# A transformer block pair on one core: an explicit list of order, engines and PSUM banks in place of a planner's priority table

## The chip, the cores and the metric

The kernel runs on 1 core of one Trainium2 chip. The metric is the device time of one execution in microseconds; the median of three runs counts.

## The reference

Two identical layers are applied twice to x (2048 tokens, 512 channels, bf16). Each layer is a windowed causal attention and an MLP, both behind a layernorm without learned scale:

```python
H = 32; Dh = D // H; W = 256                    # 32 heads of 16 channels, window of 256 keys
qkv = (x @ wqkv).reshape(B, S, 3, H, Dh)...
scores = einsum("bhqd,bhkd->bhqk", q, k) * Dh ** -0.5
mask = (i - j >= 0) & (i - j < W)
o = softmax(where(mask, scores, -1e9)) @ v ... @ wo          # attention A
h = gelu(x @ w1 + b1); y = h @ w2 + b2                       # MLP B, 512 -> 1792 -> 512
x = x + A(layernorm(x)); x = x + B(layernorm(x)); and both once more
```

## The kernel before

X (16 tiles of 128 tokens), all weights and all intermediate results stay in SBUF. The two applications are unrolled into 32 token tiles `tau` (16 for each), worked in 16 blocks `b` of two tiles. The steps of a block and the names by which the profile shows them are these.

- `layernorm`: statistics (`BATCH_NORM_STATS2` into `stat`, L786), mean and variance (`statmv`, L788), `veps` (L790), all on DVE; the power -0.5 on POOL (`rstd`, L793); the normalized tile `xn` (L796) on DVE. For attention `xn` is transposed by TensorE and copied into `xnTA` by DVE (L769) or ACT (L771). For the MLP most tiles go another way: DVE transposes into `xs_`, a DMA writes it to a scratch tensor `scr_x`, and four DMAs read it back into `xnTB` (L808, L810), all on the SP queue.
- `lnq`, `kv`: projections against `Wqkv_sb`, groups `q…`, `k…`, `v…`, and their evacuations into `QT`, `Va` (DVE, L769, or ACT, L771) and `KT` (DVE alone, L882, 128x1024).
- `attention`: 152 score groups ("visits", `QT,KT` matmuls of 32x64 tiles) into four PSUM banks each, two exponentials per group on ACT into the ring buffer `E` (L971; 304 in all), masks on `E` by DVE or POOL (L994), then `pv` groups (`E,Va` matmuls of 64x17 tiles), whose result is transposed (`TT`, L1059), divided (`Rc`, `TM`, L1062, L1064) and transposed again into `OT` (L1069).
- `outproj` against `Wo_sb`, and `residual` (`X`, L842).
- `mlp`: ten jobs of two or four tiles. W1 groups, gelu on ACT (L1133, L1143; ACT switches its function table between exp and gelu), W2 groups `W_sb,gT`, residual. For six of a job's fourteen W1 groups DVE adds the bias first (L1130) and one gelu serves two groups.

Three kinds of matmul groups therefore stand on TensorE: full-array groups (128x128), score groups (32x64 tiles) and pv groups (64x17 tiles).

Every engine runs a fixed sequence. It is made at build time: each step is `add`ed to `PL`, a `_Plan`, with its engine or engines, a duration, what it reads and writes, a priority and a class of PSUM banks. `_Plan.run` is a list scheduler: at each moment an idle engine takes the ready step with the smallest priority, where `TUNE` adds a number of its own to the priority of each step and leans the choice between two engines. Four classes of banks (`sc`, `o`, `od`, `m1`) limit which groups may use which banks; steps can also have `after`: other steps that must be planned earlier (the gates between score groups, exponentials, W1 groups and gelus). `_Sched` then turns the resulting order into the engines' programs: semaphore waits come only from what a step reads and writes, from the banks, and from `behind`, which keeps a long POOL instruction behind the last DVE instruction that uses the same port. `after` and the priorities leave no trace in the program but the order.

The loads stand at the head of the SP queue: X tiles 0-1, X 2-3, the three blocks of Wqkv (Q, K, V), b1, X 4-7, then Wo, b2, W1, X 8-15 and W2 (b2 ahead of Wo in the program).

Of the kernel before, what the change touches and what calls it, by code (L numbers as in the profile page):

```python
# [55 lines left out]
class _Sched:  # L56
# [4 lines left out]
    COUNTERS = ("pe", "act", "dve", "pool") + tuple("spdma%d" % i for i in range(N_DMA_SEMS))  # L61
# [27 lines left out]
    def op(self, eng, fn, reads=(), writes=(), inc=1, dma=False, start=0.0, end=0.0, n=1, joins=(), behind=None):  # L89
# [8 lines left out]
        if dma:  # L98
            assert eng == "sp"
            counter = "spdma%d" % (self.dma_rr % self.N_DMA_SEMS)  # L100
            self.dma_rr += 1
            inc = 16
            need(counter, self.cnt_val[counter])
# [28 lines left out]
    def wait_all_dma(self, eng):  # L132
        waits = [(c, v) for c, v in self.cnt_val.items() if c.startswith("spdma") and v]
        self.prog[eng].append(dict(fn=None, waits=waits))
# [52 lines left out]
class _Plan:  # L187
# [5 lines left out]
    TURN = {}  # L193
    LINGER = 0.0
    CODE = (194.0, 256.0, 2.003, 3300.0)

    def __init__(self, pools, tune=((), ())):
        self.keys = {}
        self.tune = tune
        self.nodes = []  # L200
        self.lw = {}
        self.lr = {}
        self.pools = pools

    def add(self, eng, fn, dur, reads=(), writes=(), prio=0.0, alloc=None, free=(), after=(), geo=None, table=None,
            dma=False, alt=(), war=(), lock=False, joins=(), chain=False):

        i = len(self.nodes)
        k = self.keys.setdefault((eng, round(prio, 3), dur), len(self.keys))
        step, lean = (float(t[k]) if k < len(t) else 0.0 for t in self.tune)  # L210
        prio += step
        alt = tuple((e2, f2, d2, h2 + 4.0 * lean) for e2, f2, d2, h2 in alt)
# [14 lines left out]
        if free and eng == "dve":  # L227
            prio -= 1000.0
        self.nodes.append(dict(
            eng=eng, fn=fn, dur=dur, reads=list(reads), writes=list(writes), prio=prio, joins=tuple(joins),  # L230
            jdeps=frozenset(self.lw[r] for r in joins),
            alloc=alloc, free=tuple(free), deps=deps, geo=geo, table=table, dma=dma, lock=lock,
            alts=((eng, fn, dur, 0.0),) + alt, key=k, done=False, behind=None, then=None,
            heavy=any(a[0] == "pool" and a[2] > 600.0 for a in ((eng, fn, dur),) + alt),
        ))
        if eng == "pe":
            c = _Count()
            fn(c, _Anywhere())
            self.nodes[i]["n"] = c.n
        if chain:  # L240
            self.nodes[i - 1]["then"] = i
        return i

    def run(self):
        import heapq
        nodes = self.nodes
        n = len(nodes)
        succ = [[] for _ in range(n)]
        indeg = [0] * n
        for i, nd in enumerate(nodes):  # L250
            indeg[i] = len(nd["deps"])
            for d in nd["deps"]:
                succ[d].append(i)
        engs = ("pe", "act", "dve", "pool", "sp")
        rtime = {e: [0.0] * n for e in engs}
        pend = {e: [] for e in engs}
        ready = {e: [] for e in engs}
        efree = {e: 0.0 for e in engs}
        locked = {"dve": 0.0, "pool": 0.0}
        last_lock = {"dve": None, "pool": None}  # L260
        held = {e: None for e in engs}
        for nd in nodes:
            nd["chained"] = False
        for nd in nodes:
            if nd["then"] is not None:
                nodes[nd["then"]]["chained"] = True
        code, edge, loaded = 2.0, self.CODE[0], 0.0
        last_geo = None
        last_tab = "exp"
        bank_free = {}  # L270
        for cands in self.pools.values():
            for c in cands:
                for b in c:
                    bank_free[b] = True
        gmap = {}

        def fit(cls):
            for c in self.pools[cls]:
                if all(bank_free[b] for b in c):
                    return c  # L280
            return None

        for i in range(n):
            if indeg[i] == 0:
                for a in nodes[i]["alts"]:
                    heapq.heappush(pend[a[0]], (0.0, i))
        events = [(0.0, -1, None)]
        order = []
        busy = {e: 0.0 for e in engs}
        left = n  # L290
        seq = n
        while left:
            if not events:
                bad = [(nodes[i]["eng"], nodes[i]["writes"][:2], nodes[i]["alloc"]) for e in engs for (_, i) in ready[e] + pend[e]]
                raise RuntimeError("plan stuck with %d left: %s" % (left, bad[:12]))
            t = events[0][0]
            while events and events[0][0] <= t + 1e-9:
                _, _, act = heapq.heappop(events)
                if act is not None:
                    for b in act:  # L300
                        bank_free[b] = True
            for e in engs:
                while pend[e] and pend[e][0][0] <= t + 1e-9:
                    _, i = heapq.heappop(pend[e])
                    for a in nodes[i]["alts"]:
                        if a[0] == e:
                            if e == "pe":
                                ready[e].append((nodes[i]["prio"] + a[3], i))
                                if nodes[i]["geo"] == "c" and self.LINGER > 0.0:
                                    heapq.heappush(events, (rtime[e][i] + self.LINGER, seq, None))  # L310
                                    seq += 1
                            else:
                                heapq.heappush(ready[e], (nodes[i]["prio"] + a[3], i))
                if efree[e] > t + 1e-9 or not ready[e]:
                    continue
                pick = None
                if held[e] is not None:
                    if (held[e] in [x[1] for x in ready[e]]):
                        pick = held[e]
                elif e == "pe":  # L320
                    best = None
                    open_r = last_geo != "f" or any(
                        nodes[i]["geo"] == "r" and not nodes[i]["done"] and fit(nodes[i]["alloc"][0]) is not None for _, i in ready[e])
                    for p, i in ready[e]:
                        nd = nodes[i]
                        if nd["done"] or nd["chained"] or (nd["alloc"] is not None and fit(nd["alloc"][0]) is None):
                            continue
                        if nd["geo"] == "c" and not open_r and t < rtime[e][i] + self.LINGER:
                            continue
# [102 lines left out]
def bass_interleave_layers__sliding_block__dense_activation_gelu__prompt_kernel(  # L432
# [67 lines left out]
    def d_act(n):  # L500
        return n * 0.832 + 52
# [722 lines left out]
```

## Time and profile before

| | |
|---|---|
| three timed runs | 477.46, 478.22 (median), 479.47 us |
| profiled execution, its span from first to last instruction | 475.1 us |
| what lies around the span, taken from the median | 3.1 us |
| busy: PE, DVE, ACT, POOL | 450.4, 369.3, 396.2, 243.7 us |
| matmuls | 8793 |
| DMA queues | 16.92 MB on the queue of the kernel's own DMAs, 11.9% of 16 engines' span |

The profile gives no time for its execution other than the span, so the span stands for it, and the difference to the median of the timed runs, 3.1 us, is what lies around it. In the lists that follow, a line gives an engine, a line of the kernel, an operation, output<-input, the number of instructions and their time; what stands behind the last bar or in square brackets is the idle time of the engine just before, and what ended it. PE is TensorE's matmuls, PEld its weight loads. PEclk is the clock that TensorE was granted.

### The profile page before, as it was taken

The page shows a single profiled execution, that of the slowest core. Times are in us where ns is not written, and L with a number is a line of the kernel's source. Part 1 is how long each engine was busy: PE and PEld are TensorE (multiplying, and loading weights), DVE is VectorE, ACT ScalarE, POOL GpSimd, SP SyncE. Part 2 cuts the span into 40 slices and gives each one's busy share as a digit, 9 for nine tenths or more (in the row PEclk, how much of TensorE's full clock was granted, in tenths as well). Part 3 has the DMA queues.
Part 4 walks back from the last instruction along what each step waited for, and adds up shares of the span by engine and source line. Part 5 has one row for each costly group of instructions (what it writes and reads, how often), then busy time and mean ns, then how long its engine had stood idle before and what let it go on. Part 6 is the DMA issues. An engine that isn't in the chain of part 4 may idle for free.

```text
span 475.1 us, 19326 instructions
## 1 busy us (share of the span) xinstructions
PE 450.4 (95%) x8793; PEld 238.2 (50%) x8793; DVE 369.3 (78%) x735; ACT 396.2 (83%) x467; POOL 243.7 (51%) x275
## 2 busy tenths in 40 slices
PE   7987799999969999999989999999999999999997
PEld 4554464665433454645434545455455553454663
DVE  4999978988877688988878789797876958793611
ACT  2799999898897988879979898879998899875352
POOL 4296726843742435661778728672275816353200
PEclk9998999999977999999999999999999999999999
DMA  8910000001010100100010000101021001102000
GB/s 255 371 51 3 4 3 1 5 18 32 3 47 3 46 3 3 48 29 20 1 48 3 30 19 25 27 3 44 3 64 31 25 23 31 53 15 57 24 22 33
DMA packets 27837, 18.14 MB, mean 38 GB/s; under 512 B 15852, under 2 KB 27244, under 8 KB 27756
## 3 DMA queue, kind: packets, MB, share of 16 engines
q1 hardware_dynamic: 27756, 16.92, 11.9%
q8 instruction: 68, 1.11, 1.0%
q14 instruction: 13, 0.11, 0.1%
HBM read 11.41 MB, written 5.51 MB: 36 GB/s over the span
## 4 chain that ended last, share of the span: by engine, by line
PE 75%; DVE 13%; DMA 4%; ACT 4%; issue 1%; SPq 1%; POOL 1%; POOLq 0%
PE ps L32 73%; ACT E L971 3%; DVE KT L882 3%; DVE stat L786 3%; DVE X L842 2%; DMA X<-in_A_x_dram 2%; DMA xnTB<-scr_x 1%; PE ps L36 1%; DVE TT L1059 1%; DVE Va L769 1%; DMA scr_x<-xs_ 1%; DVE E L994 1%; DVE xn L796 1%; SPq L810 1%; DVE QT L769 1%
## 5 line engine op out<-in xcount | busy, mean ns | idle before, releaser
L971 ACT ACTIVATE E<-ps 128x1024 bf16<-128x1024 f32 x304 | 289.9, 1029 | 34.7 <-PE ps L32 32.8
L994 POOL TENSOR_TENSOR E<-E,mask 128x512 bf16<-128x512 bf16 (+1 forms) x148 | 154.6, 1064 | 114.1 <-ACT E L971 72.7
L32 PE MATMUL ps<-W_sb,gT 128*128 128x512 bf16 x448 | 114.9, 381 | 1.6 <-DMA xnTB<-scr_x 1.3
L32 PE MATMUL ps<-xnTB,W_sb 128*128 128x512 bf16 (+1 forms) x560 | 111.8, 340 | 1.1 <-DVE KT L882 0.5
L842 DVE TENSOR_TENSOR X<-X,ps 128x512 bf16<-128x512 bf16 x64 | 43.5, 681 | 45.3 <-PE ps L32 44.5
L32 PEld LDWEIGHTS ps<-xnTB,W_sb 128*128 128x128 bf16 x560 | 52.0, 98 | 46.5 <-issue 3.9
L32 PE MATMUL ps<-QT,KT 32*64 32x320 bf16 (+4 forms) x2976 | 66.7, 262 | 7.4 <-ACT E L971 3.4
L32 PE MATMUL ps<-xnTA,Wqkv_sb 128*128 128x256 bf16 x512 | 68.2, 277 | 3.2 <-DVE KT L882 1.2
L1143 ACT ACTIVATE gT<-ps,b1T 128x512 bf16<-128x512 f32 (+1 forms) x92 | 49.3, 587 | 23.0 <-PE ps L32 23.0
L32 PEld LDWEIGHTS ps<-W_sb,gT 128*128 128x128 bf16 x448 | 39.4, 97 | 48.9 <-issue 6.3
L793 POOL TENSOR_TENSOR rstd<-veps,mhalf 128x1 f32<-128x1 f32 x64 | 37.9, 602 | 40.3 <-DVE veps L790 38.5
L32 PEld LDWEIGHTS ps<-xnTA,Wqkv_sb 128*128 128x128 bf16 x512 | 46.8, 99 | 20.1 <-issue 4.4
L32 PEld LDWEIGHTS ps<-QT,KT 32*64 32x64 bf16 x2976 | 27.7, 104 | 53.1 <-ACT E L971 31.9
L32 PE MATMUL ps<-E,Va 64*17 64x128 bf16 (+3 forms) x3872 | 50.4, 233 | 2.7 <-issue 1.6
L1059 DVE STREAM_TRANSPOSE TT<-ps 128x1024 f32<-128x1024 f32 x32 | 39.8, 1245 | 14.6 <-PE ps L32 14.1
L994 DVE TENSOR_TENSOR E<-E,mask 128x512 bf16<-128x512 bf16 (+1 forms) x114 | 47.1, 439 | 5.1 <-ACT E L971 4.5
L32 PEld LDWEIGHTS ps<-E,Va 64*17 64x17 bf16 x3872 | 39.9, 86 | 20.4 <-issue 8.0
L786 DVE BATCH_NORM_STATS2 stat<-X 128x6 f32<-128x512 bf16 x64 | 43.4, 682 | 6.3 <-DMA X<-in_A_x_dram 5.5
L1103 POOL TENSOR_TENSOR X<-X,b2b 128x512 bf16<-128x512 bf16 x32 | 37.0, 1161 | 21.7 <-DVE xn L796 13.9
L882 DVE TENSOR_TENSOR KT<-ps,parmask 128x1024 bf16<-128x1024 f32 x32 | 38.5, 1213 | 6.9 <-PE ps L32 6.6
L1130 DVE TENSOR_SCALAR gT<-ps,b1T 128x512 bf16<-128x512 f32 (+1 forms) x48 | 31.8, 667 | 11.9 <-PE ps L32 11.4
L32 PE MATMUL ps<-Wqkv_sb,xnTA 128*128 128x512 bf16 x128 | 33.1, 381 | 0.4 <-issue 0.2
(49 smaller groups left out, 324.8 us busy)
## 6 DMA issues: line engine op xcount, KB each, us to landing
W_sb<-in_B_w_dram SPq DMA_DIRECT2D x2, 1792.0 KB, 14.5
scr_x<-xs_ SPq DMA_DIRECT2D x26, 128.0 KB, 1.7
xnTB<-scr_x SPq DMA_DIRECT2D x104, 32.0 KB, 1.9
out_dram<-X SPq DMA_DIRECT2D x16, 128.0 KB, 1.7
Wqkv_sb<-in_A_wqkv_dram SPq DMA_DIRECT2D x3, 512.0 KB, 7.3
X<-in_A_x_dram SPq DMA_DIRECT2D x1, 1024.0 KB, 13.1
X<-in_A_x_dram SPq DMA_DIRECT2D x2, 256.0 KB, 2.9
X<-in_A_x_dram SPq DMA_DIRECT2D x1, 512.0 KB, 8.6
```

Of the source, the lines that this page charges most:

```text
L32: return self.e.matmul(*a, **k)
L769: return add("dve", lambda e, B: e.tensor_copy(dst(B), src(B)), 334 if two else d_psum(n), reads=reads, writes=writes + ([] if free else r ...
L786: add("dve", lambda e, B: e.bn_stats(stat6[:, k6, :], X[:, t, :]), 590, reads=["X%d" % t], writes=["st%d" % k6], prio=prio)
L793: add("pool", lambda e, B: e.tensor_tensor(out=rstd[:, k : k + 1], in0=veps[:, k : k + 1], in1=mhalf[:], op=ALU.pow), 535, reads=["ve%d" % ...
L842: add("dve", lambda e, B: e.tensor_tensor(out=X[:, t, :], in0=X[:, t, :], in1=ps[:, B[g][0], :], op=ALU.add), d_psum(512), reads=["X%d" % ...
L882: add("dve", lambda e, B, g=g, i=i: e.tensor_tensor(out=KT[:, kb, :, 2 * i : 2 * i + 2, :].rearrange("p a c q -> p a (c q)"), in0=ps[:, B[ ...
L971: last_exp[0] = add("act", lambda e, B, g_=g_, gi=gi: e.activation(E[:, 2 * gi : 2 * gi + 2, e0 : e0 + 512], ps[:, B[g_][0] : B[g_][0] + 2 ...
L994: op = lambda e, B, Ew=Ew, Mw=Mw: e.tensor_tensor(out=Ew, in0=Ew, in1=Mw, op=ALU.mult)
L1059: add("dve", lambda e, B: e.transpose(TT[:, s].rearrange("p a c q d -> p (a c q d)"), ps[:, B[g][0] : B[g][0] + 2, :].rearrange("p a n -> ...
L1103: add("pool", lambda e, B: e.tensor_tensor(out=X[:, t, :], in0=X[:, t, :], in1=b2b[:], op=ALU.add), 1110, reads=["X%d" % t, "b2b"], writes ...
L1130: add("dve", lambda e, B, g=g, fc=fc: e.tensor_scalar(out=gT[:, fc, 0:M], in0=ps[:, B[g][0], 0:M], scalar1=b1T[:, fc : fc + 1], scalar2=No ...
L1143: gelu_last[0] = add("act", lambda e, B, g=g, fc=fc: e.activation(gT[:, fc, 0:M], ps[:, B[g][0], 0:M], AF.Gelu_apprx_tanh, bias=b1T[:, fc ...
```

## The change

`_Plan` becomes `_List`. It takes three things written out: `ORDER`, the sequence of all 3294 steps, from which each engine takes its own; `TURNS`, the engine of each step that has two; and `BANKS`, the PSUM banks of each group in the order of `ORDER`. Priorities, bank classes, `TUNE` and the gates (`after` of score groups, exponentials, W1 groups and gelus) are gone, and any bank may serve any group. `_Sched` is the same but for the names of its DMA counters. `load` takes the time at which its data are expected instead of working it out, and `load_qkv(0)` (the Q block of Wqkv) is now called between X 0-1 and X 2-3. What decides the place on the SP queue is `ORDER`, though, which holds the loads too: steps 18 (X 0-1), 20 (X 2-3), 21 (K block), 19 (Q block), 22 (V block), 23 (X 4-7), then b1, Wo, X 8-15, W1, W2 and b2. So stand the loads in the built program: Q is the fourth, behind X 2-3 and K, where it was the third behind X 2-3.

Counted in the two built programs, the same steps stand on TensorE (8793 matmuls), on SP (160 instructions, the same kinds) and on ACT (304 exponentials, 98 gelu instructions with 18 table loads in all, as before). Their order and the engines of some differ:

| | before | after |
|---|---|---|
| runs of groups of one kind on TensorE (a new run wherever the kind changes) | 383 | 364 |
| of these, up to the third gelu stretch / behind it | 132 / 251 | 128 / 236 |
| masks on DVE, 128x512 / 128x256 | 98 / 16 | 112 / 27 |
| masks on POOL, 128x512 / 128x256 | 120 / 28 | 106 / 17 |
| `TM` on DVE / POOL | 19 / 13 | 14 / 18 |
| evacuations on ACT: `xnTA`, `QT`, `Va` | 11, 10, 7 | 8, 12, 10 |
| evacuations on ACT ahead of the first / third gelu | 12 / 14 | 8 / 12 |
| exponentials ahead of the first / third gelu | 44 / 118 | 44 / 118 |
| DVE instructions ahead of the first copy into `xnTB` | 115 | 95 |
| of these, statistics of one tile (`stat`, `statmv`, `veps`) | 18 | 12 |
| matmuls between the 49th and the 55th score group, full-array / pv | 8 / 196 | 41 / 260 |
| matmuls between the 37th and the 43rd score group, full-array / pv | 43 / 256 | 38 / 128 |
| matmuls from a job's last output projection to its first W1 matmul, jobs 2 to 7, least / most | 269 / 591 | 348 / 646 |

```diff
-class _Plan:
+class _List:
...
-    def __init__(self, pools, tune=((), ())):
+    def __init__(self, order, turns, banks):
+        self.order, self.turns, self.banks = order, turns, banks
...
     def run(self):
...
+        turns = iter(self.turns)
+        for nd in nodes:
+            if len(nd["alts"]) > 1:
+                nd["eng"], nd["fn"], nd["dur"] = nd["alts"][next(turns)]
...
+        for i in self.order:
+            nd = nodes[i]
...
+            if nd["alloc"]:
+                got = tuple(map(int, next(banks)))
...
+        return self.order
...
-        TUNE = ([
+        ORDER = [
+            0, 1, 18, 4, 5, 6, 7, 2, 15, 16, 8, 14, 20, 39, 40, 41, 3, 32, 33, 34, 17, 42, 43, 44, 35, 36, 76, 21,
...
+        TURNS = [
...
+        BANKS = (
+            "1 4 7 6 4 3 2 0 1 7 3412 0 5612 7 4 0123 6 4523 7 1 6 0123 6 4501 3 2 4567 2 4501 3 7 2 0167 2 5 "
...
-        PL = _Plan({
-            "sc": [(0, 1, 2, 3), (4, 5, 0, 1), (2, 3, 4, 5), (6, 7, 0, 1), (2, 3, 6, 7), (4, 5, 6, 7)],
-            "o": [(6,), (7,)],
-            "od": [(6, 7), (4, 5), (2, 3), (0, 1)],
-            "m1": [(5,), (6,), (7,), (4,), (3,), (2,), (1,), (0,)],
-        }, TUNE)
+        PL = _List(ORDER, TURNS, BANKS)
...
-        load_x(0, 2)
-        load_x(2, 2)
-        load_qkv(0)
-        load_qkv(1)
-        load_qkv(2)
+        load_x(0, 2, 2700.0)
+        load_qkv(0, 6200.0)
+        load_x(2, 2, 6900.0)
+        load_qkv(1, 8600.0)
+        load_qkv(2, 10300.0)
...
-                    writes=["ps:" + gA, "ps:" + gB], prio=pv, alloc=("sc", [(gA, 2), (gB, 2)]), geo="r", after=held + w1_last[1:])
+                    writes=["ps:" + gA, "ps:" + gB], prio=pv, alloc=[(gA, 2), (gB, 2)], geo="r")
...
-            gate_pe = (first_exp[0],) if live else ()
-            gate_act = (last_exp[0],) if live else ()
...
```

## The prediction

> **What bounds the kernel now.** I read the page first, then a table of stages, then the opening in order of time, then the groups of instructions.
>
> ```profile
> span 475.1 us, 19326 instructions
> PE 450.4 (95%) x8793; PEld 238.2 (50%) x8793; DVE 369.3 (78%) x735; ACT 396.2 (83%) x467; POOL 243.7 (51%) x275
> PE   7987799999969999999989999999999999999997
> PEclk9998999999977999999999999999999999999999
> PE 75%; DVE 13%; DMA 4%; ACT 4%; issue 1%; SPq 1%; POOL 1%; POOLq 0%
> ```
>
> TensorE is busy 95% of the span and holds 75% of the chain that ended last. But its gaps are not spread evenly: they lie in the first third of the span, and there too its clock drops. The stages say who sets the pace there (columns: stretch, its length, then busy time of each engine, granted clock, DMA share, GB/s).
>
> ```profile
> core 0: us, PE busy (x) PEld busy (x) DVE busy (x) ACT busy (x) POOL busy (x), PEclk, DMA share, GB/s
> 12.00:24.00 12.00, 10.95 (x154) 6.07 (x155) 11.33 (x29) 8.59 (x12) 3.23 (x5) 1.00 1.07 371
> 24.00:36.00 12.00, 10.62 (x203) 6.64 (x207) 12.00 (x33) 11.94 (x15) 12.00 (x15) 1.00 0.14 44
> 36.00:60.00 24.00, 18.41 (x556) 10.15 (x528) 22.78 (x44) 22.90 (x26) 16.80 (x17) 0.93 0.01 3
> 60.00:120.00 60.00, 58.15 (x1350) 34.06 (x1335) 51.06 (x105) 55.08 (x70) 31.13 (x34) 1.00 0.05 12
> 128.00:132.00 4.00, 3.29 (x154) 2.02 (x145) 3.73 (x10) 3.91 (x5) 3.67 (x6) 1.00 0.02 4
> 132.00:136.00 4.00, 1.67 (x96) 0.86 (x80) 3.41 (x6) 3.87 (x5) 3.18 (x3) 1.00 0.19 54
> 136.00:140.00 4.00, 2.72 (x56) 1.38 (x56) 3.37 (x7) 4.00 (x6) 0.91 (x1) 0.69 0.25 65
> 140.00:144.00 4.00, 3.07 (x136) 2.04 (x136) 1.73 (x6) 3.70 (x4) 0.24 (x1) 0.50 0.09 21
> 144.00:148.00 4.00, 3.94 (x51) 1.28 (x52) 2.74 (x5) 1.94 (x2) 1.15 (x1) 0.53 0.01 4
> 148.00:180.00 32.00, 31.89 (x592) 15.99 (x585) 25.35 (x48) 29.68 (x35) 12.02 (x13) 1.00 0.07 19
> 180.00:240.00 60.00, 60.00 (x1187) 30.92 (x1185) 52.55 (x109) 53.01 (x59) 33.85 (x40) 1.00 0.08 22
> 240.00:300.00 60.00, 58.27 (x1169) 28.62 (x1168) 50.23 (x97) 53.78 (x60) 42.74 (x44) 1.00 0.09 24
> 300.00:360.00 60.00, 59.20 (x1216) 30.42 (x1213) 47.45 (x89) 52.69 (x61) 29.50 (x30) 1.00 0.11 29
> ```
>
> Two regimes, then. Up to about 144 us ACT works almost without a gap (11.94 of 12, 22.90 of 24, 55.08 of 60, 3.70 to 4.00 of each 4) and TensorE waits for it, with DVE full beside it early on. From 148 us TensorE is full (31.89 of 32, 60.00 of 60) and the others have slack. So what shortens ACT's or DVE's road to the third gelu stretch moves the end; behind it only what TensorE itself saves does.
>
> **Part 1: the opening.** The new list moves the Q block behind X 2-3 and the K block, and the first K evacuation ahead of the statistics of X 4-7.
>
> ```profile
> 1.78 1.56 SPq L747 DMA_DIRECT2D Wqkv_sb<-in_A_wqkv_dram  x3
> 8.89 1.92 PE L32 MATMUL ps<-xnTA,Wqkv_sb 128*128 128x256 bf16 x16 [0.52 <-DVE xnTA L769]
> 10.65 0.61 PE L36 MATMUL ps<-ident,xn 128*128 128x128 bf16 x8
> 12.63 0.69 DVE L786 BATCH_NORM_STATS2 stat<-X 128x6 f32<-128x512 bf16 x1 [3.15 <-DMA X<-in_A_x_dram]
> 13.24 1.21 DVE L882 TENSOR_TENSOR KT<-ps,parmask 128x1024 bf16<-128x1024 f32 x1
> 15.27 0.42 PE L32 MATMUL ps<-QT,KT 32*64 32x256 bf16 x16
> 15.76 1.94 ACT L971 ACTIVATE E<-ps 128x1024 bf16<-128x1024 f32 x2 [1.69 <-PE ps L32]
> DMA to landing us min/median/max: 6.3/7.3/8.3
> ```
>
> The last row is that of the three Wqkv blocks. They are issued some 0.5 apart from 1.78 (three in 1.56), so Q lands today at 1.78 + 6.3 = 8.1, K at 2.3 + 7.3 = 9.6, V at 2.8 + 8.3 = 11.1. In the new order equally many bytes stand ahead of the second block: K lands at 8.1, Q at 9.6. The sequence on TensorE still begins with Q, so the first projection, today at 8.89, waits until 9.6: a loss of 0.7. Then follow 16 Q and 6 K matmuls of 256 columns, 8 transposes and 2 more K matmuls. The row of 16 gives (1.92 - 0.27)/15 = 0.11 each, that of 8 transposes (0.61 - 0.22)/7 = 0.056: 24 x 0.11 + 0.45 = 3.1, so K is ready at 12.7. Its evacuation starts there instead of at 13.24, where it stands behind statistics for which DVE waited 3.15. Before the first score group TensorE has 8 Q matmuls (0.9) and 6 V matmuls of 512 columns (0.22 each by a row further down, 1.3): 14.9 against 15.27. I take **-0.4**. Bounds: -1.5, if the Q block isn't late after all and the order of the code's calls held, and +2.1, if the longer wait of TensorE ahead of 9.6 also costs it what a drop of the clock cost in the row 36 to 60 (0.93, so 0.07 x 24 = 1.7) and the K evacuation gains nothing (+0.4).
>
> **Part 2: ACT's road to the third gelu.** Counted in the programs, 118 exponentials stand ahead of it in both. Of the evacuations (`xnTA`, `QT`, `Va`) behind the first exponential, 8 stood there and now 5.
>
> ```profile
> L971 ACT ACTIVATE E<-ps 128x1024 bf16<-128x1024 f32 x304 | 289.9, 1029 | 34.7 <-PE ps L32 32.8
> L771 ACT ACTIVATE QT<-ps 128x512 bf16<-128x512 f32 x10 | 6.0, 599 | 5.6 <-PE ps L32 5.5
> L786 DVE BATCH_NORM_STATS2 stat<-X 128x6 f32<-128x512 bf16 x64 | 43.4, 682 | 6.3 <-DMA X<-in_A_x_dram 5.5
> L788 DVE BATCH_NORM_AGGREGATE statmv<-stat 128x2 f32<-128x6 f32 x64 | 10.8, 172 | 0.4
> L790 DVE TENSOR_SCALAR veps<-statmv 128x1 f32<-128x1 f32 x64 | 8.7, 141 | 0.7
> ```
>
> Three less at 0.60 are **-1.8**. They go to DVE, which is full from 24 to 60, so this holds only if DVE's road shortens too. It does: 95 instead of 115 instructions stand ahead of the first copy into `xnTB`, without which the first MLP job can't start, and among the 20 are the statistics of six tiles, 6 x (0.68 + 0.17 + 0.14) = 6.0 us, now done later, when DVE has gaps. If that cover failed, the 1.8 would be zero.
>
> ACT's own gaps from 24 to 148 sum to 0.06 + 1.10 + 4.92 + 0.09 + 0.13 + 0 + 0.30 + 2.06 = 8.7 (the row 120 to 128 was full). The freer DVE can close some, by sooner evacuations and masks. The nearest rows give 0 to 8.7; I take **-1.0**, near zero, as most of them end on TensorE (32.8 of 34.7 us ahead of the exponentials).
>
> **Part 3: the starved stretch.** From 132 to 136 TensorE is busy 1.67 of 4, and right behind it runs at half its clock until 148. In the rows 136 to 148 it is busy 2.72, 3.07 and 3.94 at 0.69, 0.50 and 0.53: 0.8 + 1.5 + 1.9 = 4.2 us of matmul time lost, of which the 1.9 of the last row and at most the 1.5 of the row before it are exposed, since until about 142 ACT is full anyway. Between the 49th and the 55th score group the new list has 41 full-array matmuls where there were 8: at least 33 x 0.11 = 3.6 us more work just there. I take **-1.5**, between 0 and -3.4, as the sequence at another place (below) is thinner. The Trainium skill, "TensorE: Matmul & The Clock Gate", Part 1, says that the clock is halved after an idle window of about 3.4 us and given back after a busy one; the trace agrees in kind, with a low row ahead of the drop. By that rule a filled stretch never loses the clock, and the sum would be 1.9 lower.
>
> **Part 4: changes of form on TensorE.** 383 runs of groups of one kind become 364; behind the third gelu, where TensorE is the bound, 251 become 236.
>
> ```profile
> 118.07 0.39 PE L32 MATMUL ps<-xnTA,Wqkv_sb 128*128 128x256 bf16 x2
> 118.39 0.80 PE L32 MATMUL ps<-E,Va 64*17 64x256 bf16 x64
> 119.12 0.39 PE L32 MATMUL ps<-Wqkv_sb,xnTA 128*128 128x512 bf16 x1
> 119.44 0.43 PE L32 MATMUL ps<-QT,KT 32*64 32x64 bf16 x24
> 119.80 0.82 PE L32 MATMUL ps<-Wqkv_sb,xnTA 128*128 128x512 bf16 x3
> ```
>
> Starts tell the price. Two matmuls of 256 columns at 0.11 take 0.22 but 0.32 pass until the pv group. One of 512 takes (0.82 - 0.39)/2 = 0.22, and 0.32 pass until the score group: 0.10 again. The score group streams 512 columns in all, 0.22, and 0.36 pass: 0.14. So 15 changes less are 1.5 to 2.1, **-1.8**; the four ahead of it lie beside ACT's work and are worth nothing.
>
> **Part 5: what is costed at nothing.** Gates and bank classes leave only the order in the program; any cost of theirs is in the counts above. "Any bank" can add a wait where a group gets a bank that is evacuated late; in the rows from 148 to 360 TensorE's gaps are 0.11 + 0 + 1.73 + 0.80 = 2.6, so no more than that can be gained and more can be lost: 0, from -2.6 to +5.6 (the gaps in the 24 us from 36, 24 - 18.41, the most that any such stretch shows). W1 stands behind X 8-15 and b2 last, both needed only by the first MLP job, past 50 us. On SP a scratch write may now stand between another tile's four reads, which then wait for that write's transpose. What covers it: from a job's last output projection to its first W1 matmul stand 348 to 646 matmuls where 269 to 591 stood (jobs 2 to 7).
>
> **The sum.** -0.4 - 1.8 - 1.0 - 1.5 - 1.8 = -6.5 on a span of 475.1, so 468.6; with the 3.1 around it, 478.2 - 6.5 = **471.7**. Ends within this case: 467 to 475.8.
>
> **Rivals.**
> - *The stall moves.* Between the 37th and the 43rd score group the new list is thinner than before (38 full-array and 128 pv matmuls, where 43 and 256 stood). Then TensorE starves and loses its clock there instead: parts 2 (gaps) and 3 give nothing, and an exposed 3.4 comes on top: 471.7 + 1.0 + 1.5 + 3.4 = 477.6. For it speaks the count, against it that 38 matmuls are many more than the 8 that starved.
> - *More than counted.* The list also closes half of ACT's gaps (4.3 instead of 1.0), all of the exposed clock loss (3.4 instead of 1.5) and half of the late gaps (1.3): 471.7 - 3.3 - 1.9 - 1.3 = 465.2.
> - *Slower: the moved masks block DVE.* 25 masks go from POOL to DVE (112 and 27 there instead of 98 and 16), each multiplying two operands in SBUF while POOL does the same.
>
> ```profile
> L994 DVE TENSOR_TENSOR E<-E,mask x114: 275/415/1373, 21.4 to 422.5; 128x512 bf16<-128x512 bf16 x98, 128x256 bf16<-128x256 bf16 x16
> ```
>
> The least is 275 ns, the longest 1373: some mask has stood 1.1 us behind something. If 13 of the 25 are blocked so on the way of an evacuation for which TensorE waits, that is 14.3: 471.7 + 14.3 = 486.0. It turns the sign from six of them on (6 x 1.1 = 6.6 against 6.5). Against it: the median is 415, and POOL has 20 long instructions less to collide with. The Trainium skill, "SBUF — State Buffer", Who interferes with whom, says that a DVE instruction with two SBUF inputs and a POOL instruction that reads SBUF exclude each other for the whole instruction; the 1373 fits that, the median says that the order mostly avoids it. By that rule each moved mask is one more chance of a full block, which is this rival.
>
> That the change doesn't do what its name says is so in one point already: the Q block stands later, not earlier; part 1 counts it so.
>
> **How the numbers follow.** About 0.5%, 2.4 us, is what a measurement of this kernel tells from no change: 475.8 to 480.6. Forecast 0.57, more than counted 0.11, the stall moves 0.17, slower 0.15. Faster: the first two and a little of the third, 0.70; within 0.5%: the rest of the third, 0.15; slower 0.15. The range leaves out the slower case and the lowest tail: 464 to 479.
>
> **What would show it.** Right: first exponential at about 15.4; evacuations on ACT early down; no stretch between 128 and 148 in which TensorE is busy under 3 of 4, and no drop of PEclk there; third gelu some 4 to 5 us sooner; the rows behind it full. Wrong: a PEclk drop at about 90 to 110 us (the stall moved), DVE masks with a median far above today's 415 ns (blocked), or gaps of TensorE behind 148 us above 4 us.

## The result, and the profile after

The changed kernel takes 470.56 us (median of 4 runs, 469.54 to 471.80) where the kernel before takes 478.11 (4 runs of the same set, 477.46 to 479.47): a ratio of 0.9839, 95% interval 0.9809 to 0.9869, so 7.6 us or 1.6% faster. The prediction, 471.7 in a range of 464 to 479, was right in sign and size. Of its reasons one held: ACT's road to the third gelu is shorter, by more than was counted. Two did not come about (the opening, the starved stretch), one does not show in the time (the changes of form), and a cost that it had set at nothing takes away about as much as the change brings.

The page of the changed kernel, with the lines that answer to those of before, and its row for the loading of instructions (transfers, MB, share of 16 engines):

```profile
span 469.5 us, 19355 instructions
...
PE   7998999988969999999999999999999999999997
...
PEclk9999999999979999999999999999999999999999
...
q8 instruction: 69, 1.13, 1.1%
...
PE 69%; ACT 19%; DVE 4%; DMA 4%; SPq 2%; issue 2%; POOL 0%; DVEq 0%; POOLq 0%
```

The drop of the clock in the fourth slice is gone, the one in the twelfth and thirteenth is shorter. The same stages:

```profile
24.00:36.00 12.00, 10.85 (x263) 6.03 (x262) 11.24 (x26) 12.00 (x15) 9.18 (x9) 1.00 0.15 47
36.00:60.00 24.00, 22.63 (x625) 14.06 (x623) 23.09 (x48) 23.83 (x29) 17.47 (x17) 1.00 0.02 4
60.00:120.00 60.00, 55.91 (x1244) 30.93 (x1244) 51.26 (x111) 57.75 (x73) 34.16 (x36) 1.00 0.04 11
128.00:132.00 4.00, 3.06 (x80) 1.78 (x64) 4.00 (x8) 4.00 (x6) 2.84 (x3) 1.00 0.21 57
132.00:136.00 4.00, 1.35 (x17) 0.51 (x18) 1.75 (x5) 3.81 (x5) 1.52 (x2) 0.71 0.18 39
136.00:140.00 4.00, 3.89 (x136) 2.30 (x134) 0.75 (x1) 0.08 (x1) 0.00 (x0) 0.50 0.02 4
140.00:144.00 4.00, 4.00 (x76) 1.52 (x60) 3.19 (x5) 3.26 (x4) 1.06 (x1) 0.93 0.00 0
180.00:240.00 60.00, 58.58 (x1103) 30.18 (x1102) 46.80 (x106) 53.39 (x62) 26.89 (x31) 1.00 0.10 26
240.00:300.00 60.00, 57.55 (x1312) 29.30 (x1297) 50.46 (x101) 54.16 (x62) 31.88 (x33) 1.00 0.07 19
300.00:360.00 60.00, 58.87 (x1158) 31.24 (x1157) 50.37 (x102) 52.85 (x61) 27.21 (x30) 1.00 0.10 27
```

TensorE gains 4.2 us from 36 to 60 (22.63 against 18.41), and ACT, which sets the pace, 0.9 there and 2.7 from 60 to 120. But the starved stretch at 132 is still there, thinner than before (1.35 against 1.67), half a clock behind it and ACT idle from 136 to 140 (0.08 of 4). And from 180 to 360, where the kernel before leaves 2.5 us of gaps, this one leaves 5.0. ACT comes to its third gelu stretch sooner: the first gelu of it starts in the kernel before, in the changed one, and in the run `phase` that follows below, at

```profile
157.52 1.06 ACT L1133 ACTIVATE gT<-gT 128x1024 bf16<-128x1024 bf16 x1
...
151.34 1.84 ACT L1074 ACTIVATE gT<-ps,b1T 128x512 bf16<-128x512 f32 x3
...
148.37 1.84 ACT L1074 ACTIVATE gT<-ps,b1T 128x512 bf16<-128x512 f32 x3
```

So the change brings 6.2 us up to there, and from there to the end of the span it takes 318.2 us where 317.6 passed: nothing is gained behind it. TensorE's waits behind 156 us say by what they end (us in all, times, longest). First the changed kernel, in the last line the kernel before:

```profile
PE ps L32 <- issue: 3.1, 4, 1.1
PE ps L32 <- ACT E L908: 1.4, 1, 1.4
PE ps L32 <- DMA xnTB<-scr_x: 0.8, 3, 0.4
PE ps L36 <- issue: 0.4, 1, 0.4
...
PE ps L32 <- issue: 0.2, 1, 0.2
```

"Issue" is time in which TensorE waited for nothing that the profile shows: 3.5 us now, 0.2 before. One such wait in order of time:

```profile
207.14 0.78 PE L32 MATMUL ps<-E,Va 64*17 64x256 bf16 x62
208.97 0.20 PE L32 MATMUL ps<-E,Va 64*17 64x64 bf16 x2 [1.05 <-issue]
209.10 1.68 PE L32 MATMUL ps<-xnTB,W_sb 128*128 128x512 bf16 x7
```

A pv group stops two matmuls before its end, with nothing to wait for. Numbered from the start, such stops stand ahead of the matmuls 3916, 4172, 5706, 5961 and 6216, that is 128 or a multiple of it apart, but for a drift of a few. The transfers of 206 to 211 us, in 40 slices, are the loads of instructions alone:

```profile
DMA  0000400000000000000000000000000060000000
...
q8 instruction: 2, 0.03, 2.6%
```

Two loads, 3.5 us apart. The Trainium skill, "Runtime: NRT & Kernel Launch", Instruction fetch mechanics, says that instructions are refilled in 16 KiB blocks of 256 and that the cost is mostly hidden. The trace agrees with the block: 69 loads of 16 KB for 8793 matmuls, each with a weight load. That the cost is hidden does not hold for this kernel, as the runs below show.

### The profile page after: what moved, and what is told of

Its sections match the earlier page's. It is cut to its first block, busy times and chain, and to the rows that moved or that the text cites. A ratio compares the mean times of both kernels' runs of the same rounds, so it can differ in the third digit from the quotient of the medians.

```text
span 469.5 us, 19355 instructions
## 1 busy us (share of the span) xinstructions
PE 446.4 (95%) x8793; PEld 237.7 (51%) x8793; DVE 365.0 (78%) x753; ACT 392.6 (84%) x469; POOL 226.6 (48%) x255
## 4 chain that ended last, share of the span: by engine, by line
PE 69%; ACT 19%; DVE 4%; DMA 4%; SPq 2%; issue 2%; POOL 0%; DVEq 0%; POOLq 0%
PE ps L32 67%; ACT E L908 13%; DMA scr_x<-xs_ 2%; ACT gT L1074 2%; SPq L757 2%; PE ps L36 1%; DMA xnTB<-scr_x 1%; ACT gT L1066 1%; DVE X L789 1%; ACT L908 1%; ACT L1066 1%; DVE KT L829 1%; DVE stat L733 1%; DVE xs_ L752 0%; DVE TT L994 0%
## 5 line engine op out<-in xcount | busy, mean ns | idle before, releaser
L908 ACT ACTIVATE E<-ps 128x1024 bf16<-128x1024 f32 x304 | 286.0, 1047 | 28.8 <-PE ps L32 27.7
L929 POOL TENSOR_TENSOR E<-E,mask 128x512 bf16<-128x512 bf16 (+1 forms) x123 | 131.9, 1087 | 109.3 <-DVE E L929 50.9
L32 PE MATMUL ps<-W_sb,gT 128*128 128x512 bf16 x448 | 118.7, 381 | 2.9 <-ACT E L908 1.4
L32 PE MATMUL ps<-xnTA,Wqkv_sb 128*128 128x256 bf16 x512 | 72.7, 273 | 2.6 <-ACT xnTA L718 1.0
L32 PEld LDWEIGHTS ps<-xnTA,Wqkv_sb 128*128 128x128 bf16 x512 | 45.7, 98 | 24.0 <-issue 4.6
L929 DVE TENSOR_TENSOR E<-E,mask 128x512 bf16<-128x512 bf16 (+1 forms) x139 | 54.1, 415 | 2.4 <-ACT E L908 2.4
L999 POOL TENSOR_TENSOR TM<-TT,Rc 128x512 bf16<-128x512 f32 x18 | 19.0, 1058 | 39.2 <-DVE Rc L997 27.2
## 6 DMA issues: line engine op xcount, KB each, us to landing
X<-in_A_x_dram SPq DMA_DIRECT2D x2, 256.0 KB, 3.0
```

Of the source, the lines that this page charges most:

```text
L32: return self.e.matmul(*a, **k)
L908: add("act", lambda e, B, g_=g_, gi=gi: e.activation(E[:, 2 * gi : 2 * gi + 2, e0 : e0 + 512], ps[:, B[g_][0] : B[g_][0] + 2, :], AF.Exp, ...
L929: op = lambda e, B, Ew=Ew, Mw=Mw: e.tensor_tensor(out=Ew, in0=Ew, in1=Mw, op=ALU.mult)
L999: mul = lambda e, B: e.tensor_tensor(out=TM[:, sm].rearrange("p c q a d -> p a (c q) d"), in0=TT[:, s, :, :, :, 0:Dh].rearrange("p a c q d ...
```

## The experiments

Each kernel was timed in five rounds against the kernel before on the same chip; the medians of the latter were 478.4 to 478.8 in the sets. Theories at the start: the gain comes from ACT's road and the clock ahead of 150 us (the comparison of the traces), or in part from fewer changes of form behind it (the prediction's part 4). The instruction stream joined as a theory after the first four.

### The Q block where the change's words put it (q_second)

```diff
         ORDER = [
-            0, 1, 18, 4, 5, 6, 7, 2, 15, 16, 8, 14, 20, ... 76, 21, 77, 19, 45,
+            0, 1, 18, 4, 5, 6, 7, 2, 15, 16, 8, 14, 19, 20, ... 76, 21, 77, 45,
```

> The changed kernel with one edit: the Q block of Wqkv stands on the SP queue between X 0-1 and X 2-3, where the change's words and the order of the calls put it, instead of behind X 2-3 and the K block. Theory 1 (the prediction's part 1: the first projection waits for the Q block): the first projection starts 0.7 to 1.0 us sooner than its 9.91, the first exponential up to 1 us sooner than 15.81, and the time falls from 470.6 to about 469.6. Theory 2 (the changed kernel's trace names the copy into xnTA on ACT as what ended that wait, not the load): the first projection stays at 9.9, X 2-3 lands up to 1.5 us later, the first exponential comes at 15.8 to 16.5 and the time is 470.6 to 471.3.

470.42 us (465.43 to 471.57): the same, but the six runs lie so far apart that the time alone would not tell the 1 us of theory 1. The traces do, and theory 2 holds. In order of time, the changed kernel has:

```profile
8.77 1.09 ACT L718 ACTIVATE xnTA<-ps 128x512 bf16<-128x512 bf16 x2 [6.71 <-PE ps L36]
9.91 2.58 PE L32 MATMUL ps<-xnTA,Wqkv_sb 128*128 128x256 bf16 x22 [0.95 <-ACT xnTA L718]
13.31 1.22 DVE L829 TENSOR_TENSOR KT<-ps,parmask 128x1024 bf16<-128x1024 f32 x1
15.81 1.94 ACT L908 ACTIVATE E<-ps 128x1024 bf16<-128x1024 f32 x2 [0.16 <-PE ps L32]
```

The projections wait for two copies on ACT, which end at 9.86; the Q block is there at 9.61. With the block loaded earlier (there at 5.87) they still start at 9.68 and the first exponential at 15.72. It is a close race: in the traces of `evacs_act`, `phase_warm` and `phase116`, with the block fourth as in the changed kernel, it is the block that ends the wait, at 9.36 to 9.83.

### Six evacuations back on ACT (evacs_act)

```diff
         TURNS of the steps 75, 123, 234, 271, 363, 375 (into Va, QT, xnTA, Va, xnTA, QT; 0 stands for dve, 1 for act):
-            dve, dve, dve, dve, dve, dve
+            act, act, act, act, act, act
```

> The changed kernel's order with six evacuations that ACT had before and DVE has now (two of Va, one of QT0, one of QT2, two of xnTA, all between the first and the 33rd exponential) given back to ACT. Theory 1 (the prediction's part 2: ACT's own work sets the pace up to the third gelu): 6 x 0.6 = 3.6 us more on ACT, third gelu 3.6 us later and the time about 474.2. Theory 2 (what the new order brought is fewer waits of TensorE and a clock that doesn't drop around 42 us, not less work on ACT): under 1 us, 470.6 to 471.6.

472.83 us (471.51 to 476.09), a ratio of 0.9902 to before (0.9871 to 0.9933): 2.3 slower than the changed kernel, between the theories. Its stages from 24 to 60 us:

```profile
24.00:36.00 12.00, 9.73 (x231) 5.18 (x230) 8.38 (x18) 11.51 (x15) 8.84 (x9) 1.00 0.12 36
36.00:60.00 24.00, 19.00 (x455) 10.51 (x458) 18.03 (x34) 20.68 (x25) 12.40 (x14) 0.93 0.01 3
```

TensorE falls back to 19.00 of 24 and its clock to 0.93, as before the change, and the first gelu comes 6.4 us later (64.9 against 58.5), more than the 3.6 of the six copies; the third still comes 2.8 later (154.1 against 151.3). So where these copies are done does decide the opening, by ACT's time and by TensorE's starving. The end of this run is no clean price for it, as its blocks of instructions, which the runs below are about, end at other places too.

### One half of each order (early_before, late_before, open_before)

`early_before` takes the first 1144 steps of the kernel before, then the rest in the new order; `late_before` the new order's first 1140, then the rest in the old one; `open_before` the old order's first 440 and then the new one.

```diff
-        ORDER = [ the new order ]
+        ORDER = [ the first 1144 (440) steps of the old order ] + [ the others in the new order ]
```

> The order, engines and banks of the kernel before for the first 1144 steps (to behind the third gelu stretch), and for the rest the order of the changed kernel. Theory 1 (all of the gain lies ahead of 150 us: TensorE's work is 5.6 us ahead there and no more at the end): 478. Theory 2 (the prediction's part 4: behind the third gelu 15 changes of form less bring 1.8): 476.3.

> The mirror of the run ahead of it: the changed kernel's order for the first 1140 steps (to behind the third gelu stretch), then that of the kernel before. Theory 1 (all of the gain lies ahead of 150 us): 470.6, the gain whole. Theory 2 (1.8 of it comes from fewer changes of form behind the third gelu): 472.4.

> The order, engines and banks of the kernel before for the first 440 steps (to the first gelu, some 58 us), then the order of the changed kernel. Theory 1 (the 4.7 us by which TensorE is ahead at 60 us come from the opening and stay to the end): 475. Theory 2 (what is lost early is made good later in part, as when the whole first third was exchanged, where 4 of the 8 us stayed): 472 to 473.

474.45 (472.45 to 477.20), 477.65 (473.77 to 478.88) and 472.54 us (468.97 to 475.94). Neither half alone gives the 7.6: the late one 4.0, the early one 0.8. In the first two theory 1 fails outright (478 and 470.6 expected) and theory 2 is off by 2 and 5; in the third theory 2 holds. The runs did not test only what they were made for: a half of another order also moves every block of instructions behind it, as the next runs show.

### The same work, other block ends (phase, phase_bad)

```diff
         def clear(e, B):
-            for b in range(8):
-                r = e.matmul(ps[:, b, :], gT[:, 0, 0:P], zero, start=True, stop=True)
+            for b, c, d in [(b, c, c + 64) for b in range(8) for c in range(0, 512, 64)]:
+                r = e.matmul(ps[:, b, c:d], gT[:, 0, 0:P], zero[:, c:d], start=True, stop=True)
             return r
```

Two rounds of this clear the banks at the start, while TensorE waits for data. `phase_bad` has three pieces to a bank where `phase` has eight.

> The changed kernel with its 16 clearing matmuls of 512 columns at the start cut into 128 of 64 columns: the same columns streamed while TensorE waits for the first loads, but 112 more matmuls ahead of everything else. Theory 1 (TensorE's waits named 'issue', which in the changed kernel's trace stand at the matmuls number 1619, 2255, 3914, 4170, 5704, 5959 and 6214, that is 128 matmuls or a multiple of it apart but for a slow drift, are waits for the next block of 128 matmuls of the instruction stream, and cost where a block's end falls into short pv and score matmuls): all of these places move, the waits at 84, 112, 193, 208, 290, 300 and 313 us go or shrink, new ones come elsewhere, and since the counted blocks with under 3 us of work fall from 13 to 8, the time falls by 3 to 4.5 to 466 to 467.5. Theory 2 (these waits belong to the instructions at those places, not to their number): the waits stay where they are and the time stays at 470.5.

> The changed kernel with its 16 clearing matmuls cut into 48 pieces, so that all block ends lie 32 matmuls earlier in the work. Counted as above its short blocks lack 23.4 us in all, against 13.6 as it stands and 3.7 in the run 'phase'. Theory 1 (the waits are those for blocks of the instruction stream): slower than 470.5 by 5 to 10, 475 to 480, and with it all of the change's gain could be lost by its phase alone. Theory 2 (finer clearing matmuls are faster for another reason, such as the clock at the start): 463 to 470.

`phase`: 462.60 us (461.84 to 463.66), a ratio of 0.9671 to before (0.9641 to 0.9701), 8 us below the changed kernel by nothing but 112 more tiny matmuls (and three waits fewer, 60). `phase_bad`: 481.42 (480.32 to 485.99), 1.0081 (1.0046 to 1.0115): 11 above it, slower than the kernel before. Theory 1 holds in both by the sign and the places of the waits; the sizes lie above its forecast (8.0 against 3 to 4.5, 10.9 against 5 to 10). A gain from finer clearing as such is excluded by the second. Part of the 11 may be the clock: in `phase_bad` it is halved for 3.41 us four times, at 50, 105, 118 and 436 us, each time within 1.4 us of the end of such a stop (of 1.25 to 2.33 us). TensorE's waits behind 156 us in `phase`, which the same rows showed above for the changed kernel:

```profile
PE ps L32 <- DMA xnTB<-scr_x: 1.0, 3, 0.4
PE ps L32 <- issue: 0.3, 1, 0.3
```

and, in order of time, two of the new ones in `phase_bad`, inside a score group and a pv group:

```profile
173.34 0.40 PE L32 MATMUL ps<-QT,KT 32*64 32x192 bf16 x9
175.30 0.34 PE L32 MATMUL ps<-QT,KT 32*64 32x320 bf16 x7 [1.56 <-issue]
...
291.61 0.76 PE L32 MATMUL ps<-E,Va 64*17 64x256 bf16 x55
294.02 0.24 PE L32 MATMUL ps<-E,Va 64*17 64x128 bf16 x9 [1.65 <-issue]
```

One early wait seems to have its part in the starved stretch. In the changed kernel a score group stops for 1.19 us at 112, and the third MLP job's rows come late ever after (residual `X`, scratch write, reads, first W1 group):

```profile
113.55 0.29 PE L32 MATMUL ps<-QT,KT 32*64 32x320 bf16 x1 [1.19 <-issue]
...
117.05 0.68 DVE L789 TENSOR_TENSOR X<-X,ps 128x512 bf16<-128x512 bf16 x1
...
128.54 0.43 SPq L755 DMA_DIRECT2D scr_x<-xs_  x1
130.38 2.67 SPq L757 DMA_DIRECT2D xnTB<-scr_x  x6
...
135.68 0.58 PE L32 MATMUL ps<-xnTB,W_sb 128*128 128x512 bf16 x1 [1.57 <-DMA xnTB<-scr_x]
```

In `phase`, where the stop there lasts 0.21, each comes 2.0 to 3.1 sooner, though the order is the same:

```profile
115.05 0.69 DVE L789 TENSOR_TENSOR X<-X,ps 128x512 bf16<-128x512 bf16 x1 [0.41 <-PE ps L32]
...
125.48 0.43 SPq L755 DMA_DIRECT2D scr_x<-xs_  x1
127.33 4.30 SPq L757 DMA_DIRECT2D xnTB<-scr_x  x6
...
133.29 1.03 PE L32 MATMUL ps<-xnTB,W_sb 128*128 128x512 bf16 x2
```

Why did the new order meet the blocks so badly? The built programs tell: TensorE has 20 wait instructions of its own in the kernel before and 63 in the changed one. They count in the blocks like any other, so by matmul 2257 the block ends lie 12 matmuls earlier than before. That they count can be read from the stops: number all of TensorE's instructions in the built program, two for a matmul with its weight load and one for such a wait, and in the seven traces that hold every matmul all 26 waits of 0.14 us and more that end with "issue" stand right behind an instruction whose number, divided by 256, leaves 194, so that is where the blocks end. The drift above comes from the waits, too.

Both kernels' builders reckon with these loads: `_Plan` and `_List` carry `CODE = (194.0, 256.0, 2.003, 3300.0)`, the first block end, the instructions of a block, those of a matmul, and the ns that a block takes. 2.003 for each of 8793 matmuls leaves room for 26 waits, and the changed kernel has 63. How the list was made is not on record, but it fits the reckoned ends and not the built ones: a recount of what its blocks lack to 3.45 us gives 3.2 ahead of 150 us and 0.0 behind it with the ends that `CODE` puts, 5.5 and 6.1 with those of the built program.

Cutting each program into blocks of 256 instructions with the durations that the kernel's steps carry, and summing what each block lacks to 3.45 us (in each of the traces the closest two loads of instructions start 3.27 to 3.44 us apart), gives:

| kernel | own waits | short ahead of 150 us | short behind | time, us |
|---|---|---|---|---|
| before | 20 | 6.5 | 1.3 | 478.1 |
| early_before | 39 | 6.6 | 0.0 | 474.45 |
| open_before | 49 | 3.9 | 0.7 | 472.54 |
| late_before | 45 | 5.3 | 5.3 | 477.65 |
| changed kernel | 63 | 5.3 | 5.4 | 470.56 |
| phase | 60 | 3.6 | 0.2 | 462.60 |
| phase_bad | 53 | 8.1 | 14.3 | 481.42 |

`phase` puts the ends 16 matmuls later in the work (112 more is 16 less than a block), near where `CODE` has them. For the three kernels with the new order, time and count go together: 6.9 less short is 8.0 us less, 11.7 more is 10.9 more. The number of waits alone is not what costs: `phase_bad` has fewest of the three. The halves fit in sign: the one with nothing short behind 150 gains 4.0, the one with 5.3 only 0.8.

### The kernel before with the same cut (before_phase)

The old order, engines and banks, written out as a list, with the clearing of `phase`.

> The kernel before, its own order, engines and banks written out as a list, with its 16 clearing matmuls cut into 128 pieces, as the run 'phase' did to the changed kernel. Counted at 3.45 us for a block of 128 matmuls, the blocks of the kernel before that hold less work are short by 18.4 us in all as it stands and by 8.5 with 112 more matmuls at the start (the changed kernel: 13.6 and 3.7). Theory 1 (waits for the instruction stream are a cost of their own in both kernels): 478.4 falls by 5 to 9, to 470 to 473, and the change is worth about 8 again at this phase. Theory 2 (the gain of 'phase' came from undoing what the new order had brought on itself): 477 to 478.5, and part of what the change could have brought had been lost to the instruction stream.

478.62 us (476.92 to 480.39), a ratio of 0.9998 (0.9981 to 1.0015): theory 2. The count in this expectation was wrong. With its own 20 waits the old order is short by 6.5 and 1.3, and by 5.8 and 4.2 with the cut; 2.2 more was to be expected, none was seen. So the kernel before had its blocks already well placed: counted at sixteen phases, 8 matmuls apart, it lacks least where it stands (8.2 us in the recount, elsewhere 8.9 to 22.6), while the new order lacks 11.6 where it stands, 3.7 at best and 23.7 at worst. What `phase` undoes is what the change brought on itself: each at its best measured block ends, the new order is worth 15.5 us (478.1 to 462.6), and half of that was lost again.

### Filling the starved stretch (phase_warm, sp_pv, phase_sp)

```diff
 phase_warm: 12 matmuls of 512 columns between the score group and the first W1 group of the third job
+        PL.add("pe", lambda e, B: [e.matmul(ps[:, B["wk"][0], :], Wqkv_sb[:, 0, 0:P], ...) for i in range(12)][-1], ...)
 sp_pv and phase_sp, ORDER:
-            ... 791, 793, ... 811, ... 566, 1052, 1053, 1054, 910, 911 ...
+            ... 811, 566, 791, 793, ... 910, 911, 1052, 1053, 1054 ...   (phase_sp: 811 and 566 alone)
```

> As the run ahead of it (100 instead of 112 more matmuls at the start), and 12 matmuls of 512 columns that compute nothing are put where TensorE starves from 132.6 to 135.7 us, so that the number of matmuls behind them is the same as there. No wait is put on them. Theory 1 (the prediction's part 3: the starved stretch costs the clock, and the half clock behind it, while ACT stands idle from 136 to 140, is exposed): no drop of the granted clock behind 132 us, the stretch up to 141 us 2 to 3.4 us shorter, and the time 2 to 3.4 below that of the run ahead of it. Theory 2 (ACT sets the pace there, the half clock is hidden): clock restored, but the time within 0.5 of the run ahead of it. Theory 3 (filling alone doesn't keep the clock): the drop stays.

> The changed kernel with two small moves ahead of the third gelu stretch: two reads of the transposed rows on the SP queue (of tiles 0 and 3 of the job) ahead of the write of tile 2 for whose landing they now wait in the queue, and one pv group of 132 matmuls ahead of the first two W1 groups of the job, which wait for those reads while the pv group's data are there. Theory 1 (the starved stretch is exposed): the gap of 3.2 us at 132.5 shrinks by the 1.8 of the pv group, the drop of the clock goes or shortens, 1.5 to 3 less: 467.5 to 469. Theory 2 (ACT sets the pace until the third gelu anyway, or the pv group waits for its masks): 470.5, with ACT's idle time from 136 to 140 unchanged.

> The run 'phase' (128 pieces), and the two reads of the transposed rows (tiles 0 and 3) ahead of the write of tile 2 on the SP queue. In the profile of 'phase' the first W1 groups of the third MLP job wait about 1 us at 131.6 and 132.1, and the clock is halved for 3.4 us behind them. Theory 1 (these reads end that wait): the two waits go, the clock holds, 1 to 2.5 less than 462.6. Theory 2 (ACT sets the pace there): 462.6 within 0.5.

`phase_warm` takes 463.99 us (463.75 to 464.78), against 462.60 without the filling. Its rows:

```profile
132.00:136.00 4.00, 3.60 (x29) 1.50 (x22) 1.27 (x4) 3.12 (x4) 1.16 (x1) 1.00 0.09 21
136.00:140.00 4.00, 3.89 (x172) 2.27 (x172) 2.91 (x4) 1.87 (x3) 0.47 (x1) 1.00 0.01 4
```

The clock holds at 1.00 (`phase`: 0.60 and 0.97), so theory 3 is out, and the time is 1.4 higher. That the half clock is hidden (theory 2) is not shown by it: the twelve matmuls put off the first W1 group from 133.29 to 135.03, and the third gelu stretch starts at 148.8 instead of 148.4, so 1.3 of the 1.7 us had come back by then. `phase_sp`, 463.56 (462.80 to 464.88), gains nothing either, but it does not keep the clock: the drop comes one row later (1.00 from 132 to 136, 0.60 from 136 to 140). `sp_pv`, without the cut, takes 468.81 (468.28 to 470.19), within theory 1's 467.5 to 469, and its third gelu stretch starts 1.3 sooner (150.0); its interval, 0.9776 to 0.9839 of before, overlaps that of the changed kernel, and its waits behind 156 us that end with issue are 2.7 instead of 3.5. What the starved stretch costs stays open; no run shows more than about 1.8 for it.

### Four matmuls further (phase116)

132 pieces instead of 128.

> The run 'phase' with 116 instead of 112 more clearing matmuls at the start (132 pieces). Counted with this program's own wait instructions, behind 150 us no block of 128 matmuls holds less than 3.45 us of work (the run 'phase': 0.2 us short, the changed kernel 5.4), and ahead of it the block that ended with the longest wait of that run, 1.25 us at 124 us, is short by 0.67 instead of 1.49. Theory 1 (the count gives the waits, and that one delays the third MLP job): the wait at 124 us shrinks to about 0.5 and the time falls by 0.3 to 1.5, to 461 to 462.3. Theory 2 (ACT sets the pace there and hides it): 462.6 within 0.3.

463.52 us (461.42 to 465.36): 0.9 above `phase`, with intervals that overlap; neither theory foresaw more than 462.9. The wait that should have shrunk did not, in order of time:

```profile
125.77 0.42 PE L32 MATMUL ps<-E,Va 64*17 64x256 bf16 x24 [1.59 <-issue]
```

It was 1.01 in `phase`, so the count is not good to half a microsecond for a single block. What lengthens this load, with the reads of `xnTB` on their way just then, stays open.

## Why the prediction was right, point by point

- **Part 1, -0.4: nothing.** The first exponential starts at 15.81 where it started at 15.76. The Q block came at 9.61, as counted (9.6). The step that failed is what follows it: the projections start at 9.91, behind ACT's copies, and the K evacuation at 13.31 instead of 12.7, so it is no sooner than before (13.24).
- **Part 2, -1.8 and -1.0: right in kind, not in the sizes.** From the first exponential to the 118th ACT takes 134.2 us where it took 140.4. The three evacuations less are worth 1.1 of these 6.2, its idle time falls from 10.2 to 7.8, so by 2.4, and the same exponentials take 107.9 instead of 110.3 from start to start without the idle time, which the prediction had not counted. In part that is because one that follows another at once starts 0.92 us behind it where one alone lasts 1.03, and the breaks between them fell from 18 to 7. `evacs_act` shows that the place of these copies matters: six given back put the third gelu off by 2.8, or 0.5 each rather than 0.6.
- **Part 3, -1.5: the drop that went was the other one.** Clock and gaps at 36 to 60 us improved; the stretch at 132, which was to fill, starves as it did, for the late rows above. The "41 full-array matmuls" are there, but behind one that waits. Among the waits are those of two reads behind another tile's scratch write on the SP queue, which part 5 had named and put at nothing. And in the kernel before, 1.0 of the 2.3 us that TensorE stands idle there was not for want of full-array matmuls, but a block end inside a pv group:

```profile
133.44 0.46 PE L32 MATMUL ps<-E,Va 64*17 64x256 bf16 x31 [1.01 <-issue]
```

- The Trainium skill, "TensorE: Matmul & The Clock Gate", Part 1, was weighed in part 3: that a filled stretch keeps the clock is borne out by `phase_warm` (1.00), but the 1.9 us that were to follow did not come (463.99 against 462.60), at least not net of the filling's own time.
- Up to the third gelu the parts 1 to 3 sum to -4.7; in the traces it comes at 151.3 instead of 157.5, so 6.2 sooner. The sum was near with two of its terms, parts 1 and 3, wrong: what they did not bring, ACT's road brought, and more. That is luck.
- **Part 4, -1.8: not seen.** From the third gelu to the end pass 318.2 instead of 317.6 us. Against the fewer changes of form stand 3.5 us of issue waits where 0.2 stood, and perhaps 1.4 more: the wait above that is put down to an exponential stands at a block end, too, and in `q_second` and `sp_pv` it ends with "issue". With the ends moved (`phase`) the same stretch takes 461.0 - 148.4 = 312.6, 5.0 less than before. How much of that is fewer changes of form was not tested.
- **Part 5, 0: the term that failed.** "Gates and bank classes leave only the order in the program; any cost of theirs is in the counts above" overlooked the 43 more wait instructions on TensorE, and that the kernel's own builder carries a cost for the loading of instructions. With the order they stand in, the waits for the instruction stream and what comes of them cost 8 us here (470.56 against 462.60).
- The 3.1 us around the span were too many: in 25 executions of the kernel before it is 2.0 to 3.4, mostly 2.05, and the one profiled for the prediction, 475.1, was 1.3 below their median span. The spans of the two profiled executions differ by 5.6, the medians of the timed runs by 7.6; the stretches above are those of these two.
- **The signs.** Of those of being right, the third gelu came sooner and ACT has fewer early evacuations, but the first exponential did not come at 15.4 and the stretch from 128 to 148 still starves and loses its clock. Of those of being wrong, one came true: TensorE's gaps behind 148 us are above 4, 5.0 from 180 to 360 alone.
- **The rivals.** The masks did not block DVE: 139 of them, median 416 ns, longest 967, where it was 415 and 1373. The stall did not move to another place; it stayed. A time as slow as that of the third rival was near (481 in `phase_bad`, 486 foreseen), but by another mechanism.

The forecast of 471.7 was thus met by errors that cancel: ACT's road and the late order are better than counted, and the instruction stream took away what they bring behind the third gelu.

## What to carry to other kernels

Where a profile has waits that end with "issue" and stand a fixed number of matmuls apart, cut the program into its blocks of 256 instructions and ask which hold less than 3.5 us of work: a block that is filled with short matmuls (pv and score groups here, 128 of them in 1.6 us) is worked off before the next one is there. Any edit of the order, and any added wait, moves all block ends behind it; so judge a reordering at more than one phase, which a few more matmuls at the start gave for nothing here. Here the version that beats both kernels is the changed one with its clearing in 128 pieces: 462.6 us, 3.3% below the kernel before.

## What the runs showed of the hardware that was not expected

- In none of the fourteen traces do the loads of two blocks of 256 TensorE instructions start closer than 3.27 us (3.27 to 3.44 for the closest two of each), and 128 short matmuls are done in 1.6; the same order took 462.6 to 481.4 us by the position of the block ends alone.
- A wait instruction that stands alone counts in the block as one, a matmul with its weight load as two: 43 of them moved the ends by 12 matmuls at matmul 2257, and counted so, all 26 stops stand at a block's end to the instruction.
- Of TensorE's clock, the kernel before loses 10.0 us (median grant 0.979 in 25 executions), the changed kernel 3.3 (0.993), `phase` 0 to 2 (0.995 to 1.000). How much of it is paid is open: with the clock held by idle matmuls at 132 us the time was no lower, but these take time themselves.
